# Attention and two mixtures on one core: the rotation of the second head pair reordered, four copies on another queue, and the first expert tile's matmuls in another order

## The chip, the cores and the metric

The kernel runs on one core of a Trainium2 chip. Its engines are TensorE (PE; its weight loads are shown as PEld), VectorE (DVE), ScalarE (ACT), GpSimd (POOL) and SyncE (SP), which only issues transfers. A name with a q behind it, as SPq, is the engine's sequencer issuing DMAs. Each engine works through its own instructions in order, and semaphores order them between engines. The metric is the device time of one execution in microseconds.

## The reference

Three layers run one after the other, all in float32. Attention works on 2 batches, 8 heads, 576 positions and head size 64:

```python
def rotate(x):
    x1, x2 = (x[..., :half], x[..., half:])
    return np.concatenate([x1 * cos - x2 * sin, x1 * sin + x2 * cos], axis=-1)
q_rot, k_rot = (rotate(q), rotate(k))
scores = scale * np.matmul(q_rot, k_rot.transpose(0, 1, 3, 2))
scores = scores - np.max(scores, axis=-1, keepdims=True)
attn = np.exp(scores)
attn = attn / (np.sum(attn, axis=-1, keepdims=True) + 1e-09)
return np.matmul(attn, v).astype(np.float32)
```

Its output, 1152 tokens of 512 numbers, goes through a dense layer (512 to 2048, softplus, back to 512; called Moe1 here). The last layer (Moe2) gives each token with a positive skip score to the best of 8 experts (512 to 1024, relu, back to 512) and adds the gated result to the token: `out[do_compute] = xc + y`.

## The kernel before

**Attention.** The 16 heads of both batches are worked in 8 pairs. A pair has five units: four of 128 query rows for each of the two heads, and a unit "m" for the last 64 rows of both. One unit is: score matmuls on PE, the negative row maximum on VectorE (line 251), the exponential with its row sums on ScalarE (264), transposes of the probabilities on PE, their split into a high and a low part (copy or cast on ScalarE, subtraction on VectorE, 325, 329, 366), and the matmuls with v. All products are made of high and low parts: three matmuls in place of one, high by high, low by high and high by low. The row sums of the first two units get an epsilon on GpSimd (`norm`, 285) and a reciprocal on VectorE (286).

**Preparation of a pair.** Loads bring positions 0 to 511 of q and k of a pair into `xn`; those of the last 64 positions of all heads come at once into `rem`. `_rope` (130 to 133) rotates with four instructions: a product with the cosine, two half-wide products with the sine into a scratch tile, and an add. `rope_pair` does it for q (i = 0) or k (i = 1) of a pair; `rope_rem` does it for the last positions of several heads. Both take their scratch tile under one tag, `rtmp`, that has a single buffer, whichever engine does the work. The transposes of the rotated tiles (`tq`, 176 and 181) go into PSUM and from there, split, into `qT`, `kT` and `qm`. `stacks` (203 to 205) then copies `qT` and `kT` by DMA into the stacked tiles `qs`, `ks` and `kl` (high and low parts of q beneath one another, k's high part, k's low part), with four copies of each. The first two units of the first pair do not use the stacks; they read `qT` and `kT`.

**Order.** `run` writes the first pair's preparation at the start. After that `prepare` writes the next pair's between the units: q's rotation and k's in the first unit, the transposes in the second, v's split in the third (steps "qk", "t", "v" of PREP). For the second pair, numbered (0, 1), q is rotated on GpSimd and k on VectorE. A scheduler then sets the order on every engine, by its own estimates of durations; `issue_after` keeps a group of instructions from being placed before a given one. Tiles of one tag take turns in its buffers, so a tile waits for the last reader of the tile that had its buffer.

**Moe1 and Moe2.** Moe1 runs over blocks of 128 hidden features. Near its end the first tile of Moe2 is started between its last matmuls, in a PE order written by hand (`more`, `rest`): `hidden_mm` makes 24 matmuls into two halves (c = 0, 1; tiles mh00 and mh01), over four quarters k of the 512 inputs, the last two matmuls behind the routing's index matmuls. `relu` (898) follows on ScalarE, half by half, `turn` transposes and splits (909, 911, 912), and `result` (926) makes the second layer. Nine tiles run, each with its rows gathered by an indirect transfer from GpSimd (858) and transposed on PE (869).

Of the kernel before, what the change touches and what calls it, by code (L numbers as in the profile page):

```python
# [9 lines left out]
F32 = mybir.dt.float32  # L10
# [10 lines left out]
B, H, S, D = 2, 8, 576, 64  # L21
# [27 lines left out]
class Attention:  # L49
# [77 lines left out]
    def _rope(self, engs, out, x, tmp, cos, sin):  # L127

        e1, e2, e3 = engs
        e1.tensor_mul(out, x, cos)  # L130
        e2.tensor_mul(tmp[..., 0:32], x[..., 32:64], sin[..., 0:32])
        e2.tensor_mul(tmp[..., 32:64], x[..., 0:32], sin[..., 32:64])
        e3.tensor_add(out, out, tmp)

    def rope_rem(self, b, engs, h0=0, h1=H):
        if b not in self.rot:
# [4 lines left out]
        s = self.cst["sinr"].unsqueeze(1).to_broadcast([128, n, D])  # L141
        self._rope(engs, self.rot[b][:, h0:h1], self.rem[b][:, h0:h1], tmp, c, s)

    def rope_pair(self, b, hp, i, engs):
        p = self.pr[b, hp]
        if "rot" not in p:
            p["rot"] = self.nat.tile([128, 2, 4, 2, D], F32, name=f"rot{b}{hp}", tag="rot", bufs=1)
        tmp = self.nat.tile([128, 2, 4, D], F32, name=f"rt{b}{hp}{i}", tag="rtmp", bufs=1)
        c, s = (
            self.cst[x].rearrange("p (j d) -> p j d", d=D).unsqueeze(1).to_broadcast([128, 2, 4, D]) for x in ("cos", "sin")  # L150
        )
        rot = p["rot"][:, i].rearrange("p j h d -> p h j d")
        self._rope(engs, rot, p["xn"][:, i], tmp, c, s)
# [38 lines left out]
    def stacks(self, b, hp):  # L192

        p = self.pr[b, hp]
        qT, kT = p["qT"], p["kT"]
        p["qs"] = qs = self.wq.tile([128, 2, 512], F32R, name=f"qs{b}{hp}", tag="qs", bufs=2)
        p["ks"] = ks = self.wq.tile([128, 2, 576], F32R, name=f"ks{b}{hp}", tag="ks", bufs=2)
        p["kl"] = kl = self.wq.tile([128, 2, 576], F32R, name=f"kl{b}{hp}", tag="kl", bufs=2)
        for a in range(2):
            r = slice(64 * a, 64 * a + 64)  # L200
            for o in range(2):
                d = slice(64 * o, 64 * o + 64)
                self.nc.sync.dma_start(qs[d, a, :].bitcast(F32), qT[r, 0 if o == a else 1, :].bitcast(F32))
                self.nc.sync.dma_start(ks[d, a, :].bitcast(F32), kT[r, 0, 64 - 64 * a : 640 - 64 * a].bitcast(F32))
                self.nc.sync.dma_start(kl[d, a, :].bitcast(F32), kT[r, 1, 64 - 64 * a : 640 - 64 * a].bitcast(F32))

    def vprep(self, b, hp):
        nc, p = self.nc, self.pr[b, hp]
# [239 lines left out]
    def run(self, side=None):  # L448
        nc = self.nc
# [12 lines left out]
        self.stacks(0, 0)  # L462
        self.load_v(*pairs[1])
        with self.tc.issue_after(self.vprep(0, 0).ins):
            self.rope_rem(0, g3, 2, H)
        units = [(b, hp, u) for (b, hp) in pairs for u in self.order[b]]
        n = len(units)
        jobs = []
# [39 lines left out]
    def prepare(self, i, pairs):  # L508

        nc = self.nc  # L510
        g3 = tuple(self.eng(x) for x in self.en(i // 5, "rope"))
        z, pi = i % 5, i // 5
        if pi + 1 == len(pairs):
            return
        nxt = pairs[pi + 1]
        for step in PREP[z]:
            if step == "q":
                self.rope_pair(*nxt, 0, g3)
                if nxt == (1, 0):
                    self.load_rem(1)  # L520
            if step == "k":
                with self.tc.issue_after(self.latest.ins):
                    self.rope_pair(*nxt, 1, g3 if pi else (nc.vector,) * 3)
                if nxt == (1, 0):
                    self.rope_rem(1, g3)
            if step == "t":
                self.tq(*nxt)
                self.stacks(*nxt)
            if step == "v":
                self.vprep(*nxt)  # L530
            if step == "l" and pi + 2 < len(pairs):
                self.load_pair(*pairs[pi + 2])
                self.load_v(*pairs[pi + 2])
# [94 lines left out]
class Moe2:  # L628
# [254 lines left out]
    def hidden_mm(self, T, st, ph):  # L883
        nc, xt = self.nc, st[1]
        for k in range(4):
            w = self.early[k] if T == 0 else self.split_w(T, k)
            for z, (x, y) in enumerate(((0, 0), (1, 0), (0, 1))):
                for c in range(2):
                    yield partial(
                        nc.tensor.matmul, ph[c], lhsT=xt[x][:, 128 * k : 128 * k + 128],  # L890
                        rhs=w[:, y, 512 * c : 512 * c + 512], start=k == 0 and z == 0, stop=k == 3 and z == 2,
                    )

    def relu(self, T, st, xp, ph):
        nc, xg = self.nc, st[0]
# [19 lines left out]
    def result(self, T, st, xp, ps_y, mid=None):  # L915
# [3 lines left out]
        for c in range(4):  # L919
            if c == 3 and mid:  # L920
                mid()
            w = self.early[4 + c] if T == 0 else self.split_w(T, 4 + c)
            for j in range(2):
                for z, (x, y) in enumerate(((0, 0), (1, 0), (0, 1))):
                    o = 128 * (2 * c + j)
                    nc.tensor.matmul(  # L926
                        py, lhsT=ht[:, x, o : o + 128], rhs=w[:, y, 512 * j : 512 * j + 512],
                        start=c == 0 and j == 0 and z == 0, stop=c == 3 and j == 1 and z == 2,
                    )
        return partial(self.finish, T, xg, py, xp)  # L930

    def finish(self, T, xg, py, xp):
# [337 lines left out]
```

## Time and profile before

| | |
|---|---|
| time, median of 3 runs | 535.82 us (534.59 to 536.44) |
| time of the profiled execution | 536.4 us |
| its span | 534.6 us, mean granted clock .983 |
| PE busy | 499.3 us (93%) |
| VectorE busy | 437.1 us (82%) |
| ScalarE busy | 387.0 us (72%) |
| GpSimd busy | 195.2 us (37%) |

The span is that of the instructions of the profiled execution; its time has 1.8 us more around it. Busy shares are means over the whole span, and the stages differ: attention, then Moe1, then Moe2. The page's strip of 40 slices shows the start and the rest apart; a digit is the busy share of 13.4 us in tenths, and PEclk the granted clock in tenths of full speed:

```profile
PE   8699998978988999999999999999999999999994
PEclk9899999998999999999999999999998999999998
```

PE is least busy in the first two slices and in a few of the first 14, and its clock is below full speed in the second slice, in the tenth, near 410 us and at the end.

### The profile page before, as it was taken

Reading aid. Unit: us, or ns where it says so; the run is one execution under the profiler, and the core shown is the slowest. Engines: PE = TensorE matmul, PEld = TensorE weight load, DVE = VectorE, ACT = ScalarE, POOL = GpSimd, SP = SyncE. Lnnn points to the kernel's source line nnn. Section 1 sums busy time; section 2 is a strip of 40 time slices with the busy share of each in tenths; the row PEclk is TensorE's granted clock in tenths of the full one; section 3 lists DMA queues with packets and bytes.
Section 4 is the critical chain, followed back from the end, with each engine's and each line's share of the span. In section 5 each row is a group of like instructions: output and inputs, shape, how many; then the busy total and the mean of one; then the engine's idle time right before and its main releaser. Section 6 shows DMA issues by size and latency. Waiting matters only on the chain. (4 is left out here: it accounts for less than half of the span.)

```text
span 534.6 us, 9132 instructions
## 1 busy us (share of the span) xinstructions
PE 499.3 (93%) x2924; PEld 422.3 (79%) x2924; DVE 437.1 (82%) x866; ACT 387.0 (72%) x887; POOL 195.2 (37%) x236
## 2 busy tenths in 40 slices
PE   8699998978988999999999999999999999999994
PEld 3577877857866888889999999899987678677773
DVE  6687877799899999699998898356784889788994
ACT  2588888777877796688777768766783688677881
POOL 2877999987864420100000000001200614422332
PEclk9899999998999999999999999999998999999998
DMA  7897374354446022223324232400425604796300
GB/s 187 208 225 192 88 180 103 103 124 121 111 106 173 10 78 80 78 81 111 126 81 155 81 112 86 172 27 5 139 73 206 260 20 159 229 386 182 115 21 35
DMA packets 43015, 67.18 MB, mean 126 GB/s; under 512 B 9825, under 2 KB 24417, under 8 KB 42961
## 3 DMA queue, kind: packets, MB, share of 16 engines
q1 hardware_dynamic: 39184, 59.60, 37.6%
q0 software_dynamic: 1440, 4.20, 2.1%
q10 hardware_dynamic: 2336, 2.74, 1.6%
q8 instruction: 25, 0.41, 0.3%
q14 instruction: 30, 0.24, 0.1%
HBM read 67.30 MB, written 7.15 MB: 139 GB/s over the span
## 5 line engine op out<-in xcount | busy, mean ns | idle before, releaser
L581 PE MATMUL h<-xh,w 128*128 128x320 f32 (+2 forms) x464 | 105.3, 310 | 0.2 <-ACT P L264 0.2
L850 DVE TENSOR_TENSOR ws<-raw,ws 128x1024 fp32r<-128x1024 f32 x67 | 79.0, 1217 | 4.9 <-ACT ws L846 4.7
L622 PE MATMUL acc<-w,gh 128*128 128x512 f32 x288 | 81.2, 395 | 0.2 <-DVE pt L329 0.2
L581 PEld LDWEIGHTS h<-xh,w 128*128 128x128 f32 x464 | 77.8, 188 | 4.2 <-ACT P L264 0.4
L581 PE MATMUL h<-xl,w 128*128 128x320 f32 (+2 forms) x232 | 69.6, 308 | 0.0
L846 ACT CAST ws<-raw 128x1024 fp32r<-128x1024 f32 x67 | 66.5, 1063 | 0.5 <-DVE se L740 0.5
L686 POOL TENSOR_SCALAR sc<-lg 128x2 f32<-128x2 f32 (+1 forms) x3 | 1.0, 327 | 178.8 <-DVE lg L669 178.8
L622 PEld LDWEIGHTS acc<-w,gh 128*128 128x128 f32 x288 | 52.1, 188 | 10.2 <-ACT gh L612 0.6
L926 PE MATMUL y<-ws,hT 128*128 128x512 f32 x216 | 57.4, 404 | 1.1 <-DVE ws L850 0.5
L264 ACT ACTIVATE P<-s,m 128x576 f32<-128x576 f32 x64 | 48.0, 751 | 12.4 <-DVE m L251 12.0
L938 POOL DMA_INDIRECT out_dram<-yo,si x9 | 31.4, 3492 | 69.7 <-DVE yo L937 66.5
L251 DVE TENSOR_REDUCE m<-s 128x1 f32<-128x576 f32 x64 | 47.9, 750 | 8.0 <-PE s L243 6.8
L334 PE MATMUL t<-ct,P 128*128 128x128 f32 x288 | 45.9, 282 | 7.8 <-DVE pt L329 3.7
L412 PE MATMUL pv<-pt,vv 128*128 128x320 f32 (+1 forms) x272 | 49.8, 315 | 3.1 <-DVE x L424 2.4
L878 PE MATMUL mh<-ws,xgT 128*128 128x512 f32 x192 | 49.1, 399 | 1.4 <-DVE ws L850 1.0
L622 PE MATMUL acc<-w,gl 128*128 128x512 f32 x144 | 47.6, 393 | 0.0
L926 PEld LDWEIGHTS y<-ws,hT 128*128 128x128 f32 x216 | 39.0, 188 | 10.8 <-DVE ws L850 1.8
L596 ACT ACTIVATE y<-h 128x320 f32<-128x320 f32 (+2 forms) x58 | 25.3, 436 | 28.6 <-PE h L581 27.9
L334 PEld LDWEIGHTS t<-ct,P 128*128 128x128 f32 x288 | 34.2, 143 | 14.3 <-DVE pt L329 5.2
L412 PEld LDWEIGHTS pv<-pt,vv 128*128 128x128 f32 x272 | 40.2, 194 | 6.5 <-DVE x L424 3.6
L581 PEld LDWEIGHTS h<-xl,w 128*128 128x128 f32 x232 | 43.3, 188 | 2.1
L878 PEld LDWEIGHTS mh<-ws,xgT 128*128 128x128 f32 x192 | 35.0, 188 | 11.7 <-DVE ws L850 4.1
(266 smaller groups left out, 1113.3 us busy)
## 6 DMA issues: line engine op xcount, KB each, us to landing
raw<-in_moe_w_dram SPq DMA_DIRECT2D x68, 512.0 KB
raw<-in_moe_w_in_dram SPq DMA_DIRECT2D x16, 512.0 KB
raw<-in_moe_w_out_dram SPq DMA_DIRECT2D x16, 512.0 KB
ks<-kT SPq DMA_DIRECT2D x32, 144.0 KB
kl<-kT SPq DMA_DIRECT2D x32, 144.0 KB
qs<-qT SPq DMA_DIRECT2D x32, 128.0 KB
wr<-in_moe_w_dram SPq DMA_DIRECT2D x5, 512.0 KB
x2d<-x SPq DMA_DIRECT2D x9, 256.0 KB
```

The source lines that it names most:

```text
L251: self.latest = nc.vector.tensor_reduce(st["m"][:, a : a + 1], st["ps"][a][:, :, 0:288], axis=AX.XY, op=ALU.max, negate=True)
L264: nc.scalar.activation(P[:, 576 * a : 576 * a + 576].rearrange("p (c n) -> p c n", c=2), ps[:, :, 0:288], AF.Exp, bias=m[:, a : a + 1], ac ...
L334: nc.tensor.transpose(ps[:, 128 * i : 128 * i + 128], src, ident)
L412: nc.tensor.matmul(ps[:, 0:n], lhsT=vv[:, j, :], rhs=pt[:, x, self.place(c, i), 0:n], **se)
L581: nc.tensor.matmul(ps[c][:, 0:m], lhsT=w[:, 0, x, 128 * k : 128 * k + 128], rhs=src[:, k, c0 + m * c : c0 + m * c + m], start=z == 0, stop ...
L596: nc.scalar.activation(y[:, c], hv, AF.Abs)
L622: nc.tensor.matmul(acc[t], lhsT=g[x][:, 128 * j : 128 * j + 128], rhs=w[:, 1, y, :], start=f == f0 and z == 0, stop=f == f1 and z == 2,)
L846: hi = nc.scalar.copy(w[:, 0], raw)
L850: self.did[T, c] = hi.ins, nc.vector.tensor_sub(w[:, 1], raw, w[:, 0].bitcast(F32)).ins
L878: i = mm()
L926: nc.tensor.matmul(py, lhsT=ht[:, x, o : o + 128], rhs=w[:, y, 512 * j : 512 * j + 512], start=c == 0 and j == 0 and z == 0, stop=c == 3 a ...
L938: nc.gpsimd.indirect_dma_start(out=self.out, out_offset=bass.IndirectOffsetOnAxis(ap=si.bitcast(U32), axis=0), in_=yo, in_offset=None, bou ...
```

## The change

It has four parts.

1. `rope_rem(0)` for heads 2 to 7 on GpSimd becomes two calls: heads 2 and 3 at the old place, heads 4 to 7 placed behind the last add of q's rotation of the second pair (`self.turned_by`).
2. The rotation of k of the second pair, on VectorE, takes a scratch tile of its own from the tag "P" (three buffers, otherwise for the probabilities) in place of `rtmp`, and is written in the second unit (step "t") in place of the first.
3. The four copies into `kl` of the first pair are issued by ScalarE in place of SyncE.
4. In Moe2's first tile the last quarter's six matmuls go half by half (three into c = 0, then three into c = 1), and the first six of `result` go with the four that read the high part of hT ahead of the two that read the low.

```diff
@@ -130,7 +130,7 @@
         e1.tensor_mul(out, x, cos)
         e2.tensor_mul(tmp[..., 0:32], x[..., 32:64], sin[..., 0:32])
         e2.tensor_mul(tmp[..., 32:64], x[..., 0:32], sin[..., 32:64])
-        e3.tensor_add(out, out, tmp)
+        self.turned_by = e3.tensor_add(out, out, tmp)
 
     def rope_rem(self, b, engs, h0=0, h1=H):
         if b not in self.rot:
@@ -141,11 +141,16 @@
         s = self.cst["sinr"].unsqueeze(1).to_broadcast([128, n, D])
         self._rope(engs, self.rot[b][:, h0:h1], self.rem[b][:, h0:h1], tmp, c, s)
 
-    def rope_pair(self, b, hp, i, engs):
+    def rope_pair(self, b, hp, i, engs, own=False):
         p = self.pr[b, hp]
         if "rot" not in p:
             p["rot"] = self.nat.tile([128, 2, 4, 2, D], F32, name=f"rot{b}{hp}", tag="rot", bufs=1)
-        tmp = self.nat.tile([128, 2, 4, D], F32, name=f"rt{b}{hp}{i}", tag="rtmp", bufs=1)
+        if own:
+
+            tmp = self.wp.tile([128, 1152], F32, name=f"rt{b}{hp}{i}", tag="P", bufs=3)
+            tmp = tmp[:, 0:512].rearrange("p (h j d) -> p h j d", h=2, j=4)
+        else:
+            tmp = self.nat.tile([128, 2, 4, D], F32, name=f"rt{b}{hp}{i}", tag="rtmp", bufs=1)
         c, s = (
             self.cst[x].rearrange("p (j d) -> p j d", d=D).unsqueeze(1).to_broadcast([128, 2, 4, D]) for x in ("cos", "sin")
         )
@@ -202,7 +207,7 @@
                 d = slice(64 * o, 64 * o + 64)
                 self.nc.sync.dma_start(qs[d, a, :].bitcast(F32), qT[r, 0 if o == a else 1, :].bitcast(F32))
                 self.nc.sync.dma_start(ks[d, a, :].bitcast(F32), kT[r, 0, 64 - 64 * a : 640 - 64 * a].bitcast(F32))
-                self.nc.sync.dma_start(kl[d, a, :].bitcast(F32), kT[r, 1, 64 - 64 * a : 640 - 64 * a].bitcast(F32))
+                (self.nc.sync if b + hp else self.nc.scalar).dma_start(kl[d, a, :].bitcast(F32), kT[r, 1, 64 - 64 * a : 640 - 64 * a].bitcast(F32))
 
     def vprep(self, b, hp):
         nc, p = self.nc, self.pr[b, hp]
@@ -462,7 +467,7 @@
         self.stacks(0, 0)
         self.load_v(*pairs[1])
         with self.tc.issue_after(self.vprep(0, 0).ins):
-            self.rope_rem(0, g3, 2, H)
+            self.rope_rem(0, g3, 2, 4)
         units = [(b, hp, u) for (b, hp) in pairs for u in self.order[b]]
         n = len(units)
         jobs = []
@@ -518,9 +523,16 @@
                 self.rope_pair(*nxt, 0, g3)
                 if nxt == (1, 0):
                     self.load_rem(1)
-            if step == "k":
+            if step == "k" and pi == 0:
+
+                with self.tc.issue_after(self.turned_by.ins):
+                    self.rope_rem(0, g3, 4, H)
+            if pi == 0 and step == "t":
                 with self.tc.issue_after(self.latest.ins):
-                    self.rope_pair(*nxt, 1, g3 if pi else (nc.vector,) * 3)
+                    self.rope_pair(*nxt, 1, (nc.vector,) * 3, True)
+            if step == "k" and pi:
+                with self.tc.issue_after(self.latest.ins):
+                    self.rope_pair(*nxt, 1, g3)
                 if nxt == (1, 0):
                     self.rope_rem(1, g3)
             if step == "t":
@@ -884,12 +896,16 @@
         nc, xt = self.nc, st[1]
         for k in range(4):
             w = self.early[k] if T == 0 else self.split_w(T, k)
-            for z, (x, y) in enumerate(((0, 0), (1, 0), (0, 1))):
-                for c in range(2):
-                    yield partial(
-                        nc.tensor.matmul, ph[c], lhsT=xt[x][:, 128 * k : 128 * k + 128],
-                        rhs=w[:, y, 512 * c : 512 * c + 512], start=k == 0 and z == 0, stop=k == 3 and z == 2,
-                    )
+            order = [(z, c) for z in range(3) for c in range(2)]
+            if T == 0 and k == 3:
+
+                order.sort(key=lambda zc: zc[1])
+            for z, c in order:
+                x, y = ((0, 0), (1, 0), (0, 1))[z]
+                yield partial(
+                    nc.tensor.matmul, ph[c], lhsT=xt[x][:, 128 * k : 128 * k + 128],
+                    rhs=w[:, y, 512 * c : 512 * c + 512], start=k == 0 and z == 0, stop=k == 3 and z == 2,
+                )
 
     def relu(self, T, st, xp, ph):
         nc, xg = self.nc, st[0]
@@ -920,13 +936,16 @@
             if c == 3 and mid:
                 mid()
             w = self.early[4 + c] if T == 0 else self.split_w(T, 4 + c)
-            for j in range(2):
-                for z, (x, y) in enumerate(((0, 0), (1, 0), (0, 1))):
-                    o = 128 * (2 * c + j)
-                    nc.tensor.matmul(
-                        py, lhsT=ht[:, x, o : o + 128], rhs=w[:, y, 512 * j : 512 * j + 512],
-                        start=c == 0 and j == 0 and z == 0, stop=c == 3 and j == 1 and z == 2,
-                    )
+            order = [(j, x, y) for j in range(2) for x, y in ((0, 0), (1, 0), (0, 1))]
+            if T == 0 and c == 0:
+
+                order.sort(key=lambda o: o[1])
+            for z, (j, x, y) in enumerate(order):
+                o = 128 * (2 * c + j)
+                nc.tensor.matmul(
+                    py, lhsT=ht[:, x, o : o + 128], rhs=w[:, y, 512 * j : 512 * j + 512],
+                    start=c == 0 and z == 0, stop=c == 3 and z == 5,
+                )
         return partial(self.finish, T, xg, py, xp)
 
     def finish(self, T, xg, py, xp):
```

GpSimd's order from the rest rotation to the first pair's scale row (`remr0`, `remt`: last positions; `rot01`, `rt010`: q of the second pair; `vv01`: v's split of the second pair; `sm000`: row sums of the first two units; `rt020`: pair 3). Before:

```order
L130 TENSOR_TENSOR remr0_157<-rem0_136,cr_100 128x384
L131 TENSOR_TENSOR remt02_220<-rem0_136,cr_100 128x6x32
L132 TENSOR_TENSOR remt02_220<-rem0_136,cr_100 128x6x32
L130 TENSOR_TENSOR rot01_241<-xn01_143,cr_100 128x2x4x64
L133 TENSOR_TENSOR remr0_157<-remr0_157,remt02_220 128x384
L131 TENSOR_TENSOR rt010_242<-xn01_143,cr_100 128x8x32
L132 TENSOR_TENSOR rt010_242<-xn01_143,cr_100 128x8x32
L133 TENSOR_TENSOR rot01_241<-rot01_241,rt010_242 128x2x4x64
L95 TENSOR_SCALAR vv01_365<-vr1_112 128x10x64
L213 TENSOR_TENSOR vv01_365<-vr1_112,vv01_365 128x10x64
L285 TENSOR_SCALAR sm000_253<-sm000_253 128x4
L131 TENSOR_TENSOR rt020_510<-xn02_417,cr_100 128x8x32
```

Of the changed kernel:

```order
L131 TENSOR_TENSOR rt010_242<-xn01_143,cr_100 128x8x32
L132 TENSOR_TENSOR rt010_242<-xn01_143,cr_100 128x8x32
L133 TENSOR_TENSOR rot01_241<-rot01_241,rt010_242 128x2x4x64
L130 TENSOR_TENSOR remr0_157<-rem0_136,cr_100 128x256
L131 TENSOR_TENSOR remt04_247<-rem0_136,cr_100 128x4x32
L132 TENSOR_TENSOR remt04_247<-rem0_136,cr_100 128x4x32
L133 TENSOR_TENSOR remr0_157<-remr0_157,remt04_247 128x256
L95 TENSOR_SCALAR vv01_370<-vr1_112 128x10x64
L218 TENSOR_TENSOR vv01_370<-vr1_112,vv01_370 128x10x64
L131 TENSOR_TENSOR rt020_515<-xn02_422,cr_100 128x8x32
L132 TENSOR_TENSOR rt020_515<-xn02_422,cr_100 128x8x32
L290 TENSOR_SCALAR sm000_253<-sm000_253 128x4
```

The group for `remr0` ahead of the add of q (L133 on rot01) was 384 wide; in the changed kernel only a 128-wide one is left ahead of it (above the rows shown), and a group of 256 stands behind the add. The two products of `rt020` stand ahead of the row of `sm000`, where they stood behind it.

VectorE's order from the second unit's maxima to the low part of kT (`m00u`: maxima of unit u of the first pair; `pt000`: evictions; `rot01`, `rt011`: k of the second pair; `qT01`, `kT01`: its transposes). Before:

```order
L329 TENSOR_TENSOR pt000_264<-t0001_271,pt000_264 128x3x128
L131 TENSOR_TENSOR rt011_247<-xn01_143,cr_100 128x8x32
L132 TENSOR_TENSOR rt011_247<-xn01_143,cr_100 128x8x32
L251 TENSOR_REDUCE m001_275<-s0011_277 128x1
L133 TENSOR_TENSOR rot01_241<-rot01_241,rt011_247 128x2x4x64
L329 TENSOR_TENSOR pt000_264<-t0002_285,pt000_264 128x3x128
L251 TENSOR_REDUCE m002_349<-s0020_336 128x1
L161 SCALAR_TENSOR_TENSOR qT01_293<-tq010_295,qT01_293 128x512
L251 TENSOR_REDUCE m002_349<-s0021_351 128x1
L286 RECIPROCAL sm000_253<-sm000_253 128x4
L164 TENSOR_TENSOR kT01_294<-tq011_302,kT01_294 128x512
```

Of the changed kernel:

```order
L130 TENSOR_TENSOR rot01_241<-xn01_143,cr_100 128x2x4x64
L131 TENSOR_TENSOR rt011_293<-xn01_143,cr_100 128x8x32
L132 TENSOR_TENSOR rt011_293<-xn01_143,cr_100 128x8x32
L133 TENSOR_TENSOR rot01_241<-rot01_241,rt011_293 128x2x4x64
L334 TENSOR_TENSOR pt000_264<-t0001_271,pt000_264 128x3x128
L256 TENSOR_REDUCE m001_275<-s0011_277 128x1
L334 TENSOR_TENSOR pt000_264<-t0002_285,pt000_264 128x3x128
L291 RECIPROCAL sm000_253<-sm000_253 128x4
L256 TENSOR_REDUCE m002_354<-s0020_341 128x1
L166 SCALAR_TENSOR_TENSOR qT01_298<-tq010_300,qT01_298 128x512
L256 TENSOR_REDUCE m002_354<-s0021_356 128x1
L169 TENSOR_TENSOR kT01_299<-tq011_307,kT01_299 128x512
```

The four instructions of k's rotation stand as one group ahead of the evictions, and the reciprocal on `sm000` stands ahead of the maxima of the third unit, where it stood behind both.

ScalarE's order at the first exponential (`P000`) of the changed kernel (before, rows of `qm0`, then the exponentials, stood without transfers between):

```order
L168 CAST kT00_164<-tr00_183 128x2x64
L165 ACTIVATE qm0_103<-tr00_183 64x64
L210 DMA kl00_200<-kT00_164 64x576
L165 ACTIVATE qm0_103<-tr00_183 64x64
L210 DMA kl00_200<-kT00_164 64x576 x3
L269 ACTIVATE P000_252,sm000_253<-s0000_225,m000_232 128x576
```

The four issues for `kl00` stand ahead of the first exponential, one of them between the two small casts of `qm0`.

## Rows read from the trace of the kernel before

**Rows 1.** 20-us windows: length, busy of PE, PEld, DVE, ACT, POOL, PEclk, DMA, GB/s

```profile
140.00:160.00 20.00, 17.50 (x122) 14.79 (x120) 18.96 (x37) 15.47 (x42) 13.88 (x19) 1.00 0.33 86
...
200.00:220.00 20.00, 19.99 (x94) 16.56 (x95) 19.00 (x34) 11.34 (x21) 2.30 (x6) 1.00 0.30 106
...
400.00:420.00 20.00, 18.82 (x109) 13.51 (x107) 12.63 (x43) 7.27 (x12) 5.85 (x7) 0.91 0.55 204
```

**Rows 2.** the same columns in windows of 2 us, at the start

```profile
18.00:20.00 2.00, 0.87 (x7) 0.63 (x5) 0.43 (x1) 0.48 (x1) 1.92 (x3) 1.00 0.94 205
20.00:22.00 2.00, 0.66 (x4) 0.42 (x4) 1.24 (x3) 0.00 (x0) 0.73 (x1) 0.86 0.80 199
...
24.00:26.00 2.00, 2.00 (x11) 1.98 (x10) 1.50 (x4) 1.60 (x5) 1.83 (x3) 0.50 0.57 140
...
28.00:30.00 2.00, 2.00 (x12) 1.38 (x10) 1.76 (x3) 1.84 (x5) 2.00 (x4) 0.94 0.94 209
```

**Rows 3.** PE timeline: start, us, engine, line, operation, tiles, count [idle, releaser]

```profile
14.64 1.06 PE L237 MATMUL s<-kT,qT 64*128 64x288 f32 x6 [1.69 <-ACT P L264]
...
20.78 0.66 PE L176 MATMUL tq<-ct,rot 128*128 128x128 f32 x4 [1.91 <-POOL rot L133]
22.93 1.09 PE L176 MATMUL tq<-ct,rot 128*128 128x128 f32 x4 [1.50 <-DVE rot L133]
```

**Rows 4.** GpSimd's (POOL) timeline from 10 to 26 us

```profile
10.86 0.73 POOL L95 TENSOR_SCALAR vv<-vr 128x640 fp32r<-128x640 f32 x1 [9.42 <-DMA vr<-in_v_dram]
...
13.19 0.99 POOL L130 TENSOR_TENSOR remr<-rem,cr 128x384 f32<-128x384 f32 x1
14.13 1.03 POOL L131 TENSOR_TENSOR remt<-rem,cr 128x192 f32<-128x192 f32 x1
15.13 0.59 POOL L132 TENSOR_TENSOR remt<-rem,cr 128x192 f32<-128x192 f32 x1
...
19.47 1.26 POOL L133 TENSOR_TENSOR rot<-rot,rt 128x512 f32<-128x512 f32 x1
22.15 1.22 POOL L95 TENSOR_SCALAR vv<-vr 128x640 fp32r<-128x640 f32 x1 [1.42 <-DMA vr<-in_v_dram]
23.45 1.55 POOL L213 TENSOR_TENSOR vv<-vr,vv 128x640 fp32r<-128x640 f32 x1
25.09 0.20 POOL L285 TENSOR_SCALAR sm<-sm 128x4 f32<-128x4 f32 x1
25.38 0.72 POOL L131 TENSOR_TENSOR rt<-xn,cr 128x256 f32<-128x256 f32 x1
```

**Rows 5.** VectorE's (DVE) timeline from 14 to 26 us

```profile
14.01 0.71 DVE L130 TENSOR_TENSOR rot<-xn,cr 128x512 f32<-128x512 f32 x1
...
20.76 0.42 DVE L131 TENSOR_TENSOR rt<-xn,cr 128x256 f32<-128x256 f32 x1 [2.33 <-POOL rot L133]
...
22.11 0.68 DVE L133 TENSOR_TENSOR rot<-rot,rt 128x512 f32<-128x512 f32 x1
...
23.17 0.75 DVE L251 TENSOR_REDUCE m<-s 128x1 f32<-128x576 f32 x1
...
25.69 0.17 DVE L286 RECIPROCAL sm<-sm 128x4 f32<-128x4 f32 x1
25.78 0.66 DVE L164 TENSOR_TENSOR kT<-tq,kT 128x512 fp32r<-128x512 f32 x1
```

**Rows 6.** ScalarE's (ACT) timeline, the first exponential

```profile
13.76 0.74 ACT L264 ACTIVATE P<-s,m 128x576 f32<-128x576 f32 x1 [0.99 <-DVE m L251]
```

**Rows 7.** SyncE's DMA issues in the timeline, a copy of kl

```profile
14.69 0.59 SPq L205 DMA_DIRECT2D kl<-kT  x1
```

**Rows 8.** PE's timeline at the first tile of Moe2

```profile
414.86 1.15 PE L909 MATMUL ht<-ct,hs 128*128 128x128 f32 x8 [0.45 <-ACT hs L898]
...
416.92 3.06 PE L926 MATMUL y<-ws,hT 128*128 128x512 f32 x12 [0.22 <-DVE hT L912]
420.38 0.63 PE L869 MATMUL xgt<-ct,xg 128*128 128x128 f32 x4 [0.40 <-DMA xg<-x2d,gi]
```

## The prediction

> **What bounds the kernel now.** I read the windows of 20 us first, because they say where time can be won or lost at all. From 200 us on TensorE (PE) is full: 19.99 of 20.00 us [rows 1]. An instruction that VectorE, ScalarE or GpSimd does earlier there buys nothing; only the stretch 400 to 420, with 18.82 us and a granted clock of .91, has something left. Of the attention, which ends near 195 us, no engine is full over a whole window: in 140:160 PE is busy 17.50 and VectorE 18.96 us [rows 1]. So a delay at the start may be carried to the hand-over, and may also be partly made good.
>
> Three of the four edits lie between 12 and 28 us, so windows of 2 us come next [rows 2]. PE is busy only 0.87 us of 18:20 and 0.66 of 20:22, and then its clock falls: a mean of .86 in 20:22 and of .50 in 24:26, with .94 in 28:30. If the low level is .50 (1.2 GHz), .86 puts the fall at 22 − (.14/.50) × 2 = 21.4 us and .94 the recovery near 28.2. The DMA share is .94 in 18:20.
>
> The timelines of the single engines name the waits. PE stands 1.69 us for ScalarE's first exponential, 1.91 us for GpSimd's rotation add of q and 1.50 us for VectorE's rotation add of k [rows 3]. GpSimd has no hole from 13.19 until q's add ends at 19.47 + 1.26 = 20.73; after that it waits 1.42 us for v's load and does the value split (1.22 + 1.55) before the tiny scale row at 25.09 [rows 4]. That row adds the row sums' epsilon; VectorE's reciprocal, behind it in VectorE's order, needs it. VectorE's wait of 2.33 us ends with GpSimd's q add only because both rotations share one scratch buffer [rows 5].
>
> **Edit 1, q ahead of later rows.** GpSimd now rotates heads 2 and 3 alone before q, and heads 4 to 7 behind q. The old group was .99 + 1.03 + .59 + .99 = 3.60 us (the last .99 is the group's add, 384 wide like its first product) [rows 4]. Rows of 256, 384 and 512 elements last .72, .99 and 1.26 us, .27 per 128; carried on, an estimate, 128 elements take .45 and 64 take .32. Heads 2 and 3 so cost 2 × .45 + 2 × .32 = 1.54 us, and q is ready at 20.73 − 2.06 = 18.7 us. Heads 4 to 7 cost 2 × .72 + 2 × .45 = 2.34 us (the halves are 128 wide), to 21.0; then the value split, .73 to 1.22 + 1.55, to 23.3 to 23.8. Its loads should have landed: they come up behind fewer issues on SyncE. In the new order two 256-wide products of pair 3's rotation (.72 + .73) stand ahead of the scale row, which stood ahead of them before. The scale row then ends at 23.3 + 1.45 + .20 = 24.95, or 25.45 with the longer split, against 25.29 before. Saving q's wait has not made this row earlier.
>
> **Edit 2, k's own buffer.** VectorE's rotation of k no longer waits for GpSimd: .71 + .42 + .42 + .68 = 2.2 us [rows 5], where the row of .42 stands for two. It runs while GpSimd works, so both read memory together. The traced case is 14.13: GpSimd's 192-wide product took 1.03 us beside VectorE's .71 us product and the next one .59 alone [rows 4, 5], .44 us for one overlap. For four instructions of VectorE I take 0 to 1.8 us more on GpSimd, and .4 in the sum, since only the first of them would meet a GpSimd row squarely, as traced. The scale row then ends at about 25.4.
> The Trainium skill's rule (SBUF — State Buffer, Who interferes with whom) is harsher: a two-input VectorE instruction and GpSimd lock each other out of a shared port pair until the first is done. By it all 2.2 us of the rotation would be added to GpSimd's path and the scale row would end near 27. The .44 us beside a .71 us partner agrees with a lock only in part, so the sum does not use it.
>
> The price is in VectorE's order. Before, the reciprocal stood behind the maxima of unit 2's two heads and the low half of qT, and came at 25.69 [rows 5], when the scale row was done: no wait. Now it stands directly behind the evictions of unit 1, ahead of the maximum that came at 23.17 [rows 5]. I follow the chain to it. Edit 3 (below) delays the first exponential by 1.5 us; the next score matmuls at 14.64 [rows 3] go to 16.1, their maximum to 17.4, k's rotation to 18.2 to 20.2, then eviction, maximum and eviction, to about 21.9. There VectorE stands for the scale row until 25.4, some 3.5 us, with four things queued behind it: unit 2's maxima, qT's low half, kT's low half and so the next scores. Reciprocal .17, then the maximum at 25.6 instead of 23.17. The wait that PE imposed on the second maximum is gone, so kT's low half comes at 25.6 + .75 + .68 + .76 = 27.8 instead of 25.78 [rows 5]: +2.0 us. PE, whose transposes of k began at 22.93 with hardly a hole behind them, runs out of scores until about then.
>
> So two PE waits of 1.91 and 1.50 us go, and what is late next is the reciprocal. Bounds: if GpSimd is undisturbed and the split short, the scale row ends at 24.95 and the shift is 1.5 us; with 1.8 us of disturbance it is 3.3. Value: **+2.0 us**. A pair takes many times that, but the order is the same in every pair, so I carry the shift on to 195 us.
>
> **Edit 3, four copies on ScalarE's queue.** They stand ahead of the first exponential, in ScalarE's in-order stream, one between the two small casts and three behind. One such issue costs SyncE .59 us [rows 7]. Of four (2.4 us) the hole of .99 us before the exponential [rows 6] hides part: 1.4 us are left. Three of the four also reuse a transfer slot that a load or another copy must free first; hence 1.5, with 0.5 (issues that cost half) and 3 (a slot that comes late) as bounds. In the forecast the reciprocal's wait swallows this delay; without that wait it would stand by itself. SyncE gets on 4 × .59 = 2.4 us sooner, but the transfers are already at .94 of the engines [rows 2], so I count nothing for it.
> The Trainium skill (DMA: Bandwidth & Descriptors, Issuing engines are not separate DMA queues) says that a second issuing engine saves issue time only. The share of .94 with SyncE alone agrees; by the rule the saving is at most those 2.4 us of issuing.
>
> **Edit 4, the first tile.** PE waits .45 us for the first half's activation and .22 us for VectorE's low half [rows 8]; half c0 now finishes two matmuls sooner and the low parts are asked for later, so both may go. But the next thing on PE that cannot be early is tile 1's transposition at 420.38, which already waits .40 us for its gathered rows [rows 8]; GpSimd issues these, and that issue does not move. PE would wait there instead. Bounds −.67 and +.2 (one activation beside another matmul order); value 0.
>
> **Sum.** 536.4 + 2.0 + 0 = 538.4 us for the profiled execution (span 534.6 and 1.8 us around it). The median of the runs shown is 535.82, .58 less, so I say **537.8 us**; its own range is 536.5 to 540.5.
>
> **Rivals.**
> *Nothing is left of it.* The shift is made good before 195 us: in 140:160 PE idles 2.5 us of 20 [rows 1], and a late start need not last if loads or another pair's hand-over set the pace. For it: no engine is full. Against it: VectorE at 18.96 of 20 cannot catch up fast. Time: 535.8, within ±1.6.
> *Faster: the low-clock stretch goes.* If the scale row is early enough (its split is moved up by 1.42 us of ended wait, and the two products ahead of it shrink), the reciprocal does not hold VectorE. Then q at 18.7 and k at 20.2 let PE transpose both without the 1.91 and 1.50 us, VectorE's 23.17 maximum comes about 1.3 us earlier, and PE, which did full windows at the low clock, gets about 1 us back. It decides when the scale row ends before some 23.3 us, which needs 1.65 us less on GpSimd than the least I count. Time: 535.8 − 2.3 = 533.5.
> *Slower still: two low-clock stretches.* ScalarE's issues lengthen PE's first hole from 1.69 to about 3.2 us, and the reciprocal makes a second one. PE did 2.00 of 2.00 us in a window at .50 [rows 2]; another 4 us of work at that level costs up to 2 us. Time: 537.8 + 2 = 540.
>
> **How the numbers follow.** Stall at the reciprocal .42, two low stretches .08, nothing left .28, faster .22. Hence faster .22, same .28, slower .50; within .3% (1.6 us) this kernel's measurement cannot tell a change. The range that should hold 8 of 10 leaves out the far part of the faster case and of the slowest: 533.3 to 540.6.
>
> **What would show it.** In the changed kernel's profile: GpSimd's add of q near 18.7; its scale row near 25.4, behind two products; a VectorE reciprocal with an idle of 3 us or more ahead of it, released by GpSimd; ScalarE's first exponential near 15.3 with four transfer issues ahead; PE without holes only after 26 us and the low clock up to 30 or later; and at 420 us a longer PE wait for the gathered rows. It is wrong if the reciprocal has no idle ahead of it, if the clock stays high through 22 to 28 us, or if the pairs after the second stand where they stood before.

## The result, and the profile after

| | before | after |
|---|---|---|
| median | 535.38 us (534.43 to 537.47, 8 runs) | 540.18 us (537.54 to 542.65, 8 runs) |
| ratio | 1 | 1.0076 (1.0048 to 1.0103) |
| profiled execution: span | 534.6 us | 539.5 us |

The change makes the kernel 4.1 us slower by the ratio (2.6 to 5.5). In the profile after, lines of the kernel stand 5 to 19 numbers higher. ScalarE's timeline at the first exponential, which answers [rows 6, 7], where the exponential starts at 13.76 and an issue takes .59 us (columns as in [rows 3]):

```profile
12.60 0.51 ACTq L210 DMA_DIRECT2D kl<-kT  x1
...
13.45 3.32 ACTq L210 DMA_DIRECT2D kl<-kT  x3
16.82 0.74 ACT L269 ACTIVATE P<-s,m 128x576 f32<-128x576 f32 x1 [3.44 <-DMA kl<-kT]
```

Three issues of `kl` and the waits between them occupy ScalarE's queue for 3.32 us, and the first exponential comes at 16.82, 3.06 us late, right behind the last of them (16.77). VectorE's two maxima were done at 14.93, so they did not hold it. The second and the third of these issues, shown alone:

```profile
14.47 0.96 ACTq L210 DMA_DIRECT2D kl<-kT  x1
...
16.23 0.54 ACTq L210 DMA_DIRECT2D kl<-kT  x1
```

The three issues last .54, .96 and .54 us; the other 1.28 us (.48 and .80) are waits. In the trace the issues of SyncE and ScalarE take eight completion semaphores in turn, and ScalarE's issues here each wait for the semaphore that they are going to use, until the transfer that had it before has landed (all its data has arrived). By the trace's semaphore events a load of v, issued by SyncE at 11.31, had landed at 14.45, and a copy into `qs`, issued by SyncE at 12.53, at 16.21; the two issues above had to follow them on the same semaphores. SyncE gained nothing from having four copies fewer: its eight took from 11.90 to 19.22, where the twelve had taken from 11.55 to 19.11, and the load of v behind them was issued at 19.27 (19.16 before).

PE's timeline, which answers [rows 3]:

```profile
12.41 1.07 PE L242 MATMUL s<-kT,qT 64*128 64x288 f32 x12
17.70 1.80 PE L242 MATMUL s<-kT,qT 64*128 64x288 f32 x6 [4.22 <-ACT P L269]
...
20.91 1.81 PE L242 MATMUL s<-kT,qT 64*128 64x288 f32 x6
...
23.34 1.06 PE L181 MATMUL tq<-ct,rot 128*128 128x128 f32 x4
...
25.16 1.05 PE L181 MATMUL tq<-ct,rot 128*128 128x128 f32 x4
...
28.19 0.52 PE L339 MATMUL t<-ct,P 128*128 128x128 f32 x3 [1.29 <-DVE qT L166]
...
30.75 0.28 PE L417 MATMUL pv<-pt,vv 128*128 128x256 f32 x1
```

The scores start .54 us later than before. That is not put down to the change: in the kernels below they start anywhere from 11.20 to 12.34. PE's hole before its third group of scores is 4.22 us, where it was 1.69. The groups behind it then last 1.80 us, where they lasted 1.06: the clock has fallen. The waits for q's and k's rotation are gone, as meant, but they are gone because PE comes late. The windows, which answer [rows 2]:

```profile
16.00:18.00 2.00, 0.30 (x1) 0.30 (x2) 0.00 (x0) 1.18 (x3) 1.84 (x4) 0.50 0.96 250
18.00:20.00 2.00, 2.00 (x9) 1.72 (x9) 0.46 (x1) 0.37 (x2) 2.00 (x3) 0.50 0.91 221
...
24.00:26.00 2.00, 2.00 (x10) 1.98 (x9) 1.12 (x2) 1.36 (x4) 2.00 (x3) 0.50 0.90 244
26.00:28.00 2.00, 0.90 (x6) 0.66 (x5) 1.37 (x4) 0.53 (x2) 1.62 (x4) 0.96 0.53 159
```

PE runs at .50 from 16 to about 26 us, with full windows from 18 on; before it was 21.4 to 28.2. GpSimd and VectorE, answering [rows 4, 5]:

```profile
13.68 0.45 POOL L130 TENSOR_TENSOR remr<-rem,cr 128x128 f32<-128x128 f32 x1
...
17.87 1.27 POOL L133 TENSOR_TENSOR rot<-rot,rt 128x512 f32<-128x512 f32 x1
...
20.73 1.06 POOL L133 TENSOR_TENSOR remr<-remr,remt 128x256 f32<-128x256 f32 x1
22.25 0.74 POOL L95 TENSOR_SCALAR vv<-vr 128x640 fp32r<-128x640 f32 x1 [0.46 <-DMA vr<-in_v_dram]
...
24.90 0.72 POOL L131 TENSOR_TENSOR rt<-xn,cr 128x256 f32<-128x256 f32 x1
...
26.39 0.20 POOL L290 TENSOR_SCALAR sm<-sm 128x4 f32<-128x4 f32 x1
```

```profile
20.33 0.87 DVE L130 TENSOR_TENSOR rot<-xn,cr 128x512 f32<-128x512 f32 x1
21.12 0.95 DVE L131 TENSOR_TENSOR rt<-xn,cr 128x256 f32<-128x256 f32 x1
...
22.44 1.09 DVE L133 TENSOR_TENSOR rot<-rot,rt 128x512 f32<-128x512 f32 x1
...
24.58 0.54 DVE L334 TENSOR_TENSOR pt<-t,pt 128x384 fp32r<-128x384 f32 x1
26.63 0.18 DVE L291 RECIPROCAL sm<-sm 128x4 f32<-128x4 f32 x1 [1.50 <-POOL sm L290]
26.72 0.72 DVE L256 TENSOR_REDUCE m<-s 128x1 f32<-128x576 f32 x1
...
28.82 0.69 DVE L169 TENSOR_TENSOR kT<-tq,kT 128x512 fp32r<-128x512 f32 x1
```

GpSimd's add of q ends at 19.14, the scale row starts at 26.39 behind two products, and the reciprocal waits 1.50 us for it. The maximum behind it comes at 26.72, 3.55 us later than before; kT's low half 3.04 us. At the first tile, answering [rows 8]:

```profile
419.99 0.66 PE L925 MATMUL ht<-ct,hs 128*128 128x128 f32 x4 [0.25 <-ACT hs L914]
...
424.90 0.63 PE L881 MATMUL xgt<-ct,xg 128*128 128x128 f32 x4 [1.14 <-DMA xg<-x2d,gi]
```

Where does it go? I compare profiles by stretches, each worked out from two rows of PE's timeline: from the first scores to the first 320-wide matmul of Moe1 (before: 11.87 and 216.09), from there to the logits of the first tile, and from these to the index matmuls. A part of the first stretch is given too, from the first scores to the transposes of pair 3, which are these rows before and after:

```profile
42.58 0.60 PE L176 MATMUL tq<-ct,rot 128*128 128x128 f32 x4
```

```profile
46.08 0.60 PE L181 MATMUL tq<-ct,rot 128*128 128x128 f32 x4
```

| kernel | ratio of times (95%) | scores to pair 3 | scores to Moe1 | logits to index |
|---|---|---|---|---|
| before | 1 | 30.7 | 204.2 | 8.33 |
| after | 1.0076 (1.0048 to 1.0103) | 33.7 | 207.6 | 9.09 |
| only_kl: edit 3 | 1.0046 (1.0026 to 1.0065) | 33.2 | 207.5 | 6.79 |
| kl_on_sync: 1, 2, 4 | 1.0002 (.9972 to 1.0033) | 30.9 | 205.1 | 8.85 |
| own_buf: edit 2 | 1.0008 (.9984 to 1.0032) | 30.6 | 204.6 | 6.79 |
| q_first: edit 1 | 1.0038 (1.0007 to 1.0069) | 32.8 | 207.2 | 9.19 |
| only_t0: edit 4 | .9976 (.9955 to .9998) | 30.4 | 204.3 | 6.79 |
| kl_late | 1.0047 (1.0018 to 1.0076) | 32.4 | 207.1 | 6.80 |
| eps_dve | 1.0058 (1.0034 to 1.0081) | 33.6 | 206.4 | 8.96 |
| after_fill | 1.0008 (.9981 to 1.0035) | 31.1 | 205.5 | 8.33 |
| eps_dve_sync | .9986 (.9965 to 1.0007) | 29.7 | 203.8 | 9.17 |
| sync_fill | .9979 (.9953 to 1.0005) | 28.9 | 203.2 | 6.79 |
| t0_fill | 1.0025 (1.0007 to 1.0042) | 32.7 | 206.4 | 6.79 |
| before_again | 1.002 (.9998 to 1.0041) | 30.2 | 203.5 | 6.80 |

The middle stretch, Moe1, is 189.0 or 189.1 us in every one. Of the 4.9 us between the two profiled spans, .54 stand ahead of the scores, 3.4 in the attention and .8 between logits and index. The last is chance (below). Of the attention's 3.4 us, 3.0 are there by pair 3, so the loss is made at the start and carried on.

Two cautions go with the table. Each stretch is read from one execution, and before and before_again, the same program, differ by .7 us in the attention and by .002 in the ratio; smaller differences are not to be read. And the scheduler answers an edit with another order on every engine. Compared instruction by instruction with the kernel before, PE's order differs in 61 to 68 places, most of them in the attention, in after, only_kl, q_first, kl_late, eps_dve, after_fill and sync_fill, and in 2 to 8 in the others (none in before_again). That order alone is not the loss, since after_fill and sync_fill have it; a share of it is not excluded.

### The profile page after: what moved, and what is told of

Its sections match the earlier page's. It is cut to its first block, busy times and chain, and to the rows that moved or that the text cites. A ratio compares the mean times of both kernels' runs of the same rounds, so it can differ in the third digit from the quotient of the medians.

```text
span 539.5 us, 9128 instructions
## 1 busy us (share of the span) xinstructions
PE 500.0 (93%) x2924; PEld 424.3 (79%) x2924; DVE 436.6 (81%) x866; ACT 388.3 (72%) x887; POOL 194.5 (36%) x240
## 5 line engine op out<-in xcount | busy, mean ns | idle before, releaser
L608 ACT ACTIVATE y<-h 128x320 f32<-128x320 f32 (+2 forms) x58 | 25.4, 438 | 26.4 <-PE h L593 25.7
```

Of the source, the lines that this page charges most:

```text
L608: nc.scalar.activation(y[:, c], hv, AF.Abs)
```

## The experiments

Theory A: the issues on ScalarE delay the first exponential, and that sets the attention. Theory B, the prediction's: the reciprocal ahead of the maxima does.

**kl_on_sync**, the changed kernel with the copies back:

```diff
-                (self.nc.sync if b + hp else self.nc.scalar).dma_start(kl[d, a, :]...
+                self.nc.sync.dma_start(kl[d, a, :]...
```

> The changed kernel with the four kl copies back on SyncE's queue (edits 1, 2 and 4 stay). Theory A (the issues on ScalarE cost most: three of them took 3.32 us and the first exponential came at 16.82 instead of 13.76): the first exponential is back near 13.8 to 14.3, PE's hole of 4.22 us shrinks to about 1.7, the low clock shortens from about 11 to about 7 us, and the time falls by 3 to 4 us, to within 1.6 us of the kernel before. Theory B (the reciprocal in front of the maxima costs most): VectorE stands 3 us or more for the scale row and the time stays 2 us or more above the kernel before (ratio 1.004 or more).

Measured 1.0002, an interval apart from that of the changed kernel. The first exponential is at 14.20, PE's hole 1.70 us. Theory A holds for its size; theory B's 2 us or more are not there, and the reciprocal waits .94 us, not 3. Its first product with v comes 15.4 us behind the first scores (16.7 before), but pair 3's transposes 30.9 us (30.7 before): the gain of 1.3 us is given back between. PE's timeline there:

```profile
32.51 0.50 PE L248 MATMUL s<-kl,qs 128*128 128x288 f32 x2 [0.35 <-DMA kl<-kT]
...
35.54 0.50 PE L248 MATMUL s<-ks,qs 128*128 128x288 f32 x2 [0.80 <-DMA ks<-kT]
```

PE waits for the stacks of pair 2, which it does not there in the kernel before, and GpSimd at 37.67 waited 2.48 us for the next load (.46 before). So transfers seem to take the place of the rotation; that they set the pace was not tested.

**only_kl**, the kernel before with edit 3 alone, its diff the reverse of the one above.

> The kernel before with edit 3 alone. Theory A: the first exponential comes near 16.8, PE's first hole is about 4 us, and the time is 3 to 4.5 us above the kernel before (ratio 1.0055 to 1.0085). Theory B: the late exponential is hidden behind the wait for q's rotation (1.91 us) and k's (1.50 us), and the time is at most 1.6 us above the kernel before.

Measured 1.0046 (2.5 us), a hole of 4.65 us, and nearly all of the attention's loss (3.3 us). The median lies below theory A's band and above theory B's 1.6 us, the interval touches both. Edit 3 is enough for most of the loss; the wait for q does not hide it. It does not separate the late exponential from the reciprocal, though: the scheduler moved the reciprocal ahead of unit 2's maxima here too, and it waited.

```profile
26.59 0.18 DVE L286 RECIPROCAL sm<-sm 128x4 f32<-128x4 f32 x1 [1.29 <-POOL sm L285]
```

**only_t0**, edit 4 alone.

> The kernel before with edit 4 alone. The prediction's account: PE's waits of .45 and .22 us at 414 to 417 go, the wait for the gathered rows at 420 grows by as much, and the time stays within 0.7 us (ratio .9987 to 1.0013). Rival: the shorter holes keep PE's clock up at 407 to 412 or let tile 1 start sooner, and the time falls by 1 us or more.

Measured .9976, just below the expected band and by the rival's amount. PE's two cited waits did change as the prediction's account has it, .45 to .25 us and the second gone, and the wait for the gathered rows grew from .40 to 2.04 us. In the changed kernel it grew to 1.14. The clock did stay up between logits and index, as the rival has it (6.79 us), but so it did in the second profile of the kernel before (6.80), without the edit. Whether the 1.3 us are the edit's is open: before_again, with no edit, lies nearly as far from 1, and kl_on_sync, which has the edit too, does not show them.

**own_buf**, edit 2 alone.

> The kernel before with edit 2 alone (own scratch buffer for k's rotation on VectorE, written a unit later). Theory A: VectorE's wait of 2.33 us for GpSimd's add and PE's wait of 1.50 us for k go, nothing else is late, the time falls by 0 to 1.5 us (ratio .997 to 1.000). Theory B: the reciprocal, which stands one place earlier and behind only one maximum, holds VectorE by 1 to 2 us and the time rises by 0.5 to 2 us (ratio 1.001 to 1.004).

Measured 1.0008, no difference. VectorE's wait for GpSimd's add is gone, but PE waits 2.48 us for q, and the reciprocal .21 us. The buffer alone moves nothing that can be measured; PE's wait is for q, which this edit leaves where it was.

**q_first**, edit 1 alone.

> The kernel before with edit 1 alone (q's rotation ahead of the rotation of heads 4 to 7). If the wait for q (1.91 us) sets the second pair's end, pair 3's transposes come 1 to 2 us earlier and the time falls by 1 us or more (ratio at most .998). If k, the scale row or the copies into the stacks take its place, the time stays within 0.8 us (ratio .9985 to 1.0015), with the reciprocal, which now stands ahead of the maxima, waiting for GpSimd.

Measured 1.0038, slower than both accounts by its median (its interval reaches into the second's band). VectorE shows two waits:

```profile
21.26 0.43 DVE L131 TENSOR_TENSOR rt<-xn,cr 128x256 f32<-128x256 f32 x1 [1.33 <-POOL remr L133]
...
23.98 0.18 DVE L291 RECIPROCAL sm<-sm 128x4 f32<-128x4 f32 x1 [0.90 <-POOL sm L290]
```

Without its own buffer k's rotation waits for the scratch tile of heads 4 to 7, which now stand between (`POOL remr`, 1.33 us), and the reciprocal, ahead of the maxima as expected, .90 us. Together with edits 2 and 4 it measured 1.0002, which fits that edit 1 needs edit 2; the two intervals overlap, so it is not shown.

**kl_late**, the four copies on ScalarE's queue behind the first unit's exponentials:

```diff
+            if i == 0:
+                with self.tc.issue_after(self.first_exp.ins):
...
+                            nc.scalar.dma_start(p["kl"][d, a, :]...
```

> The changed kernel, but the four kl copies on ScalarE's queue stand behind the first unit's two exponentials. Theory A1 (an issue waits until the copy that used its completion slot has landed, and the copies of ScalarE stood too near those of SyncE; place decides): the first exponential is back near 14, the issues behind it take about 0.5 us each because the slots are free by then, and the time is within 1.6 us of the kernel before (ratio at most 1.003). Theory A2 (two queues issuing at once share one issuer, an issue costs 1.1 us on either): the four issues still take 3.5 to 4.5 us, they now delay the casts and exponentials behind them, and the time stays 2 us or more above (ratio 1.004 or more).

Measured 1.0047. The rows of ScalarE and of VectorE:

```profile
15.27 1.26 ACTq L517 DMA_DIRECT2D kl<-kT  x2
...
16.58 1.77 ACTq L517 DMA_DIRECT2D kl<-kT  x2
18.39 0.48 ACT L372 COPY pw<-t 128x384 f32<-128x384 f32 x1 [2.29 <-DMA ks<-kT]
```

```profile
26.57 0.18 DVE L292 RECIPROCAL sm<-sm 128x4 f32<-128x4 f32 x1 [2.29 <-POOL sm L291]
```

The first exponential is back at 14.22. One by one the issues last .51, .71, .61 and .47 us, nearer to theory A1's .5 than to 1.1, and ahead of the last stands a wait of .69 us until a `ks` copy, issued by SyncE at 15.00, had landed (17.86). The copy behind them waits 2.29 us in all. So the waits are for landings, as in the changed kernel; why single issues take up to .96 us beside SyncE's, a shared issuer or another cause, is open. Theory A1's time did not come: VectorE stood 2.29 us for the scale row, theory B's wait. The first product with v is only .2 us later than in the kernel before (16.9 and 16.7 us behind the first scores), pair 3 is 1.7 us late; which wait makes that was not tested.

**eps_dve**, the changed kernel with the scale row's add on VectorE:

```diff
-        nc.gpsimd.tensor_scalar(sums[:, 5 : 5 + n], sums[:, 0:n], 1e-9, 1.0, ...
+        (nc.gpsimd if b + hp + c else nc.vector).tensor_scalar(sums[:, 5 : 5 + n], ...
```

> The changed kernel with the epsilon add of the first scale row on VectorE in place of GpSimd, so that the reciprocal no longer waits for GpSimd; the copies stay on ScalarE's queue. Theory B (the reciprocal's wait, 1.50 us in the changed kernel, is carried on): the first product with v comes about 1.5 us earlier than in the changed kernel (29.3 instead of 30.75) and the time falls by 1 to 2 us (ratio to the kernel before 1.004 to 1.006 in place of 1.0076). Theory A (the late first exponential alone): the maxima behind the reciprocal are then held by PE's scores, and the time stays at 1.007 to 1.008.

Measured 1.0058 against 1.0076, intervals that overlap. The wait at the reciprocal is gone; the first product with v comes .7 us earlier behind the first scores, not 1.5, and the attention is 1.2 us shorter, of which .7 can be chance. So B's wait is at most the smaller part, and that it is carried on is not shown.

**after_fill**, the changed kernel with idle matmuls in the hole:

```diff
+            if u == 0 and a == 1:
+                self.fill(16, t)
```

> The changed kernel with 16 idle matmuls (of zeros, into a bank of their own) in PE's first hole, 13.5 to 17.7 us. Clock theory (the low clock from 16 to 26 us is what makes the delay as long as it is): the granted clock stays 1.00 until about 20 us or longer, scores and transposes of the first two units run at 1.06 and 1.24 us in place of 1.80 and 1.54, and the time falls by 1 to 2.5 us. Rival: the delay is set by ScalarE's and VectorE's waits, which the clock does not move, and the time stays within 0.7 us of the changed kernel (ratio 1.006 to 1.009).

Measured 1.0008: nearly all of the loss is gone, more than expected. The first two units' work at full clock:

```profile
12.54 3.63 PE L460 MATMUL fill<-warm 128*128 128x512 bf16 x16
16.14 1.05 PE L242 MATMUL s<-kT,qT 64*128 64x288 f32 x6
...
17.93 1.06 PE L242 MATMUL s<-kT,qT 64*128 64x288 f32 x6
...
19.31 0.60 PE L181 MATMUL tq<-ct,rot 128*128 128x128 f32 x4
...
22.09 0.63 PE L181 MATMUL tq<-ct,rot 128*128 128x128 f32 x4 [1.65 <-DVE rot L133]
```

```profile
18.00:20.00 2.00, 2.00 (x16) 1.84 (x16) 1.98 (x3) 1.80 (x6) 2.00 (x4) 1.00 0.95 211
```

The first exponential is still late (3.7 us behind the first scores, 4.4 in the changed kernel, 1.9 before). Scores last 1.06 and 1.05 us again, and q is transposed right behind them; the granted clock of 22:24 is 1.00 too. From the first scores behind the hole to the end of q's transposes PE needs 3.8 us where it needed 6.7, which is what the low clock cost it there. But the fill changed one more thing. The scheduler put the reciprocal behind unit 2's maxima and kT's low half, so that its wait no longer holds them:

```profile
25.96 0.18 DVE L293 RECIPROCAL sm<-sm 128x4 f32<-128x4 f32 x1 [1.01 <-POOL sm L292]
```

So the run takes away the low clock and theory B's order together, and what each is worth is not separated. Nor does the low clock always cost time: in before_again it begins some 5 us earlier than in the kernel before, and PE comes to q's transposes at the same 8.9 us behind the first scores, because there it waits for q in either case (.39 and 1.91 us).

**eps_dve_sync** and **sync_fill**: edits 1, 2 and 4, the add on VectorE, copies on SyncE; the second with `self.fill(7, t)` at the same place.

> As eps_dve, with the kl copies back on SyncE's queue: edits 1, 2 and 4, no wait of VectorE for GpSimd at the reciprocal. If the reciprocal's 0.94 us wait seen with the copies on SyncE is what eats the gain of edits 1 and 2, the time falls 1 us or more below the kernel before (ratio .998 or less). If pair 2's copies in the stacks set the pace (PE waited .35 and .80 us for them at 32 to 36 us), the time stays within 0.7 us of it.

> Edits 1, 2 and 4 with the copies on SyncE's queue, the epsilon add on VectorE, and 7 idle matmuls in PE's first hole (1.70 us). Clock theory: the low clock of 15.5 to 21 us goes or shrinks to half, pair 3's transposes come 0.5 to 1.5 us earlier from the first scores than with the same kernel without them (29.7 us), and the time is 1.5 to 3 us below the kernel before (ratio .994 to .997): a version that beats both. Rival: the pair's stack copies and loads set the pace, the clock is up and the time stays at .998 to 1.000.

Measured .9986 and .9979: neither can be told from the kernel before. The attention is the shortest of all in sync_fill, 203.2 us (203.5 in before_again), and pair 3's transposes come 28.9 us behind the first scores (30.7 before). This is the best version found, at most 2.5 us faster by its interval, and not shown to be faster at all.

eps_dve and eps_dve_sync are also the clearest pair for edit 3. They differ in the queue of the four copies alone, in neither does the reciprocal wait, and they measured 1.0058 and .9986, intervals apart: some 3.9 us for edit 3 with theory B's wait out of the way (and with the scheduler's other order, as said above).

**t0_fill**, edit 4 and 8 idle matmuls ahead of q's transposes.

> The kernel before with edit 4 and 8 idle matmuls in PE's hole ahead of q's transposes (1.91 us at 18.9). Clock theory: the low clock of 21.4 to 28.2 us goes or gets shorter and the time falls 0.5 to 1.5 us against edit 4 alone (ratio .995 to .997 in place of .9976). Rival: what the kernel before does at the low clock lies beside VectorE's and ScalarE's work, and the time stays at .997 to 1.000.

Measured 1.0025, against both accounts. The clock fell before the idle matmuls began (.95 in 14:16, .50 in 16:18), so these ran slowly, 3.24 us, and ended after q was ready; VectorE's reciprocal, moved ahead of the maxima by the new order, waited 2.07 us. Which of the two made the loss is open.

**before_again**, every edit undone.

> The order of the kernel before, every edit undone, looked at a second time. Chance theory: whether PE's clock falls behind the same first hole of 1.69 us (it did in five of eight profiles with that hole), and whether it falls between the logits and the index matmuls of the first tile (8.3 to 9.2 us there in place of 6.8), differs from one execution to the next: one of the two differs from the first profile (fall at 21.4 us; 8.33 us), and the time is 535 to 537 us all the same. Rival: both belong to the order of a kernel, and the second profile shows them as the first.

Measured 536.14 us, a ratio of 1.002 (.9998 to 1.0041) for one and the same order on every engine. The same program, another execution:

```profile
16.00:18.00 2.00, 1.85 (x9) 1.58 (x8) 0.61 (x2) 1.67 (x6) 1.92 (x3) 0.64 0.91 230
18.00:20.00 2.00, 2.00 (x9) 1.59 (x8) 0.26 (x1) 0.48 (x1) 1.92 (x3) 0.50 0.94 208
```

```profile
404.29 1.95 PE L671 MATMUL lgp<-w,x2T 128*128 128x9 f32 x16
...
411.09 0.39 PE L802 MATMUL idx<-oht,ohp 128*128 128x17 f16 x9
```

The clock fell near 16.6 us and not at 21.4, and there was no fall between logits and index (6.80 us, 8.33 in the first profile). Both are chance from one execution to the next, 1.5 us at the first tile.

## Why the prediction was right, and where it was not

The sign and the range held, and the profile shows most of the steps. The size was half of the measured one, and the main term was another. That is in part luck: the sum rests on the reciprocal's wait and has nothing for edit 3's delay, which makes most of the loss, and 540.18 us lies only .4 us inside the range.

- *q's rotation, 18.7.* Right: it ended at 19.14 in a profile that starts .54 us later. The small products took .45 and .31 us (.45 and .32 forecast).
- *The scale row, 25.4.* Within its bounds: it ended at 26.59, or 26.05 on the earlier start, behind the two products of pair 3. That v's loads would have landed was wrong: GpSimd waited .46 us for one, since SyncE issued it no earlier.
- *The reciprocal's wait, some 3.5 us.* Its place was right, its size not: 1.50 us, because VectorE's evictions ended at 25.12 and not at 21.9. Removed, it gave at most 1.2 us of attention, not 2.0.
- *The delay on ScalarE, 1.5 us, swallowed by the reciprocal.* This step failed. The first exponential came 3.06 us late, .54 of it the later start, so 2.5 for a term of 1.5; the bounds were .5 and 3. The issues themselves were priced about right (2.6 us for four, 2.4 forecast). The wait for a transfer slot, which the sum names and gives .1 us, measured 1.28. And the delay was not swallowed: alone edit 3 makes 2.5 us, and without it the change measures as before. The 2.4 us that SyncE was to save, counted as nothing, were nothing.
- *The clock.* I gave two low stretches a chance of .08 and 540 us. One long stretch came, and 540.18 us. With the clock held up by the fill most of the loss was gone, but the reciprocal's place changed with it; how much of the loss is the clock's stays open.
- *The shift carried on to 195 us.* Right: 3.0 us at pair 3, 3.4 at the end of the attention.
- *"Nothing is left of it" for edits 1 and 2.* The rival's mechanism fits what happened to their gain: 1.3 us at the first product with v, gone by pair 3, with waits for the copies of pair 2 between.
- *Edit 4, no gain.* Its waits moved to the gathered rows as forecast; the changed kernel shows no gain from it, and edit 4 alone is open.

## What to carry to other kernels

An issue put into a computing engine's stream can cost, besides its own duration, the wait until the transfer that had its completion semaphore before has landed, and everything behind it on that engine waits too. Ask which earlier transfer that is, and when it lands. When a hole ahead of the matrix engine grows, price the low clock that can follow it with the delay itself, from rows at either level. A stall removed in one pair should be followed to the same place of the next pair: here PE then waited for transfers. And where a scheduler sets the order, an experiment with one edit is not one change: compare the engines' orders before a difference is put down to the edit.

## What the runs showed of the hardware

The clock's fall is not set by the order of the program alone: before and before_again have the same order on every engine. With the same first hole of 1.69 to 1.70 us, PE kept its clock past 20 us in three profiles (the kernel before, own_buf, only_t0) and lost it between 14.4 and 16.9 us in six (kl_on_sync, kl_late, eps_dve_sync, q_first, t0_fill, before_again). The runs of one kernel spread over 3 to 7 us; how much of that is the clock was not measured.

VectorE and GpSimd slowed each other more than I took from one row. In kl_on_sync:

```profile
18.39 1.33 POOL L133 TENSOR_TENSOR rot<-rot,rt 128x512 f32<-128x512 f32 x1
...
20.55 0.90 POOL L131 TENSOR_TENSOR remt<-rem,cr 128x128 f32<-128x128 f32 x1
```

```profile
18.52 1.48 DVE L132 TENSOR_TENSOR rt<-xn,cr 128x256 f32<-128x256 f32 x1
20.04 1.10 DVE L133 TENSOR_TENSOR rot<-rot,rt 128x512 f32<-128x512 f32 x1
```

The half-wide product of k took 1.48 us, .42 when alone, and ended .28 us behind GpSimd's add; GpSimd's 128-wide product took .90 us beside VectorE's add, .45 when alone. That agrees with the lock that the Trainium skill states (SBUF — State Buffer, Who interferes with whom) better than the .44 us I had weighed it by.
